# Testing for a wait once per run of V-product rounds, and no filler matmuls, in a one-core decode attention kernel

## The chip, the cores and the metric

The kernel runs on one core of a Trainium2 chip. The metric is device time in microseconds (us) for one execution. The profile's span, from the first to the last instruction, is some 1.4 to 2.8 us shorter than that. The core has a matrix engine (PE), a vector engine (DVE), a scalar engine (ACT), POOL, and SP, which here issues nearly all loads. The trace records the clock granted to PE, as 1 (full) or 0.5 (half); "mean clock" is its average over the span.

## The reference, cut to what matters

One token goes through layer norm, attention with grouped heads over a cache of 65,536 positions, a residual, a second layer norm and a gated feed-forward block. There are 32 query heads on 8 key and value heads of width 128.

```python
q = (layernorm(x) @ wq)                    # 32 heads of 128
scores = einsum("bhqd,bhkd->bhqk", q, k) * Dh ** -0.5
p = softmax(scores)                        # over 65536 positions
o = einsum("bhqk,bhkd->bhqd", p, v)        # the "V product"
h = x + o.reshape(...) @ wo
h2 = h + (sigmoid(g) * u) @ w_down         # g, u: layernorm(h) @ w_gate, w_up
```

K and V are 134 MB each in bf16, and each byte is used once.

## The kernel before

SP loads K and V in pieces of 8 or 12 chunks (4.19 or 6.29 MB) into one ring in SBUF, the on-chip memory. DVE transposes K, PE makes scores, ACT exponentiates, DVE transposes the probabilities, and PE makes the V product of head h-1 while the scores of head h are made. A load of a new piece is issued when the old contents of its place in the ring have been used, so a late PE or DVE makes a late issue.

PE's program is a loop over heads with four parts in each. Parts 0 and 3 hold rounds of the V product: ten and six rounds of eight matmuls. Three kinds of filler matmul, whose results nobody reads, keep PE occupied.

```python
def warm(e, n=1, load=True):               # n fillers of 128 x 504, into an unused bank of PSUM, where PE's results go
    ...
label("values", "part")
e.reg_mov(m, PARTS[0])                     # 10 rounds; part 3 sets 6
warm(e, 3)                                 # filler 1: ahead of each of the four parts
...
goto("sums", "values")
pv_regs(e)                                 # 14 address registers of this round
...
away("br_eq", p, c, "waits", waits, "products")   # in EVERY round: is a wait due?
goto("products", "sums")
section("B")                               # the 8 matmuls
mm_at(e, ps(5, 0, 504, 96, 128), ..., kept=True)  # filler 2: one in every round
e.reg_alu(p, p, s, ALU.add)
...
e.reg_alu(m, m, -1, ALU.add)
e.br_ne(m, 0, on_true="sums", on_false="sums_end")
label("sums_end")
def outs():
    warm(e, 2); section("O"); warm(e, 1, load=False)   # filler 3: around a head's output
```

The tests ask whether the next rounds need a V piece that may not have landed: after six rounds of part 0, and, for the last head only, after four of part 3.

## Time and profile before

| | kernel before |
|---|---|
| time, median of 6 runs | 657.7 us (657.62 to 659.03) |
| span of the profiled run | 656.2 us |
| bytes read, mean rate | 282.33 MB, 430 GB/s |
| PE busy, mean clock | 460.9 us, 0.872 |
| filler matmuls | 128 in the rounds, 121 elsewhere |

The times fall into two groups, near 657.6 and near 658.9 us.

This is the timeline of PE's weight loads in the last part of the last head. The columns are start in us, duration in us, engine, line, operation and operands, count, and in brackets the idle time before.

```profile
637.41 0.17 PEld L415 LDWEIGHTS PS<-ring,PT_sb 128*32 x8 [1.09 <-issue]
638.52 0.17 PEld L415 LDWEIGHTS PS<-ring,PT_sb 128*32 x8 [0.95 <-issue]
639.68 0.17 PEld L415 LDWEIGHTS PS<-ring,PT_sb 128*32 x8 [1.00 <-issue]
640.80 0.17 PEld L415 LDWEIGHTS PS<-ring,PT_sb 128*32 x8 [0.95 <-issue]
```

A round starts 1.11 to 1.16 us after the one before it. The eight weight loads take 0.17 us. "issue" means that the profile shows nothing that PE waited for: here its own sequencer works through registers and branches. In the round that starts at 469.29 us, for one, the trace records six register operations of 36 to 79 ns and two branches, of 226 and 75 ns.

### The profile page before, as it was taken

What the parts mean: (1) busy time and instruction counts of PE and PEld (TensorE: products, weight loads), DVE (VectorE), ACT (ScalarE), POOL (GpSimd) and SP (SyncE); (2) the same over time, 40 slices, a digit from 0 to 9 for tenths busy, and PEclk for the clock granted to TensorE, in tenths of its full rate; (3) what the DMA queues carried; (4) which work ended last, traced back from release to release, by engine and by line L of the source; (5) the groups of instructions that cost most, each with busy time, mean ns of one, the idle gap of its engine ahead of it and who ended that gap; (6) DMA issues with size and microseconds to landing.
All of it is one profiled execution on the core that took longest, in us unless ns stands there. A gap on an engine that the chain in (4) does not pass through costs nothing.

```text
span 656.2 us, 6578 instructions
## 1 busy us (share of the span) xinstructions
PE 460.9 (70%) x2564; PEld 73.8 (11%) x1587; DVE 350.2 (53%) x432; ACT 42.9 (7%) x114; POOL 3.6 (1%) x17
## 2 busy tenths in 40 slices
PE   0688587857669567786677676695767966777776
PEld 0200010011001010010100111010100101001122
DVE  1299846747266645647258380684536572573202
ACT  1100200020000200001000200002000020001001
POOL 1000000000000000000000000000000000000000
PEclk9989799788889697896887988787978978879798
DMA  9999999999999999999999999999999999999998
GB/s 400 431 447 431 425 421 431 431 437 433 455 431 431 431 415 434 440 443 433 421 447 431 431 423 447 446 434 437 399 447 431 431 431 431 460 434 411 425 429 348
DMA packets 8498, 282.33 MB, mean 430 GB/s; under 512 B 1073, under 2 KB 1074, under 8 KB 1586
## 3 DMA queue, kind: packets, MB, share of 16 engines
q1 hardware_dynamic: 8354, 282.33, 99.6%
q10 hardware_dynamic: 144, 0.00, 0.0%
HBM read 282.33 MB, written 0.00 MB: 430 GB/s over the span
## 4 chain that ended last, share of the span: by engine, by line
DMA 54%; PE 26%; DVE 12%; issue 6%; ACT 1%; PEldq 0%; PEld 0%; SPq 0%
DMA ring<-in_A_k_cache_dram 33%; PE PS L415 22%; DMA ring<-in_A_v_cache_dram 19%; DVE ktw L504 11%; DMA x_col<-in_A_x_dram 2%; PE PS L423 2%; ACT P_sb L550 1%; PE PS L817 0%; DVE PT_sb L560 0%; DVE M_sb L511 0%; PE PS L660 0%; PEldq L171 0%; PE PS L835 0%; PE PS L386 0%; PE PS L544 0%
## 5 line engine op out<-in xcount | busy, mean ns | idle before, releaser
L504 DVE STREAM_TRANSPOSE ktw<-ring 128x1024 f32<-128x1024 f32 x256 | 292.3, 1207 | 152.2 <-DMA ring<-in_A_k_cache_dram 152.2
L415 PE MATMUL PS<-ktw 128*128 128x512 bf16 x1024 | 287.1, 430 | 103.2 <-DVE ktw L504 86.0
L415 PE MATMUL PS<-ring,PT_sb 128*32 x1024 | 90.5, 423 | 52.6 <-PEq L171 26.8
L415 PEld LDWEIGHTS PS<-ktw 128*128 x256 | 26.7, 104 | 343.6 <-issue 246.4
L415 PE MATMUL PS<-qz,PT_sb 128*32 128x504 bf16 x128 | 53.1, 415 | 0.0
L415 PEld LDWEIGHTS PS<-ring,PT_sb 128*32 x1024 | 25.0, 115 | 134.7 <-issue 131.0
L593 ACT ACTIVATE po_sb<-PS,rl 128x512 bf16<-128x512 f32 x8 | 5.5, 687 | 524.1 <-PE PS L415 524.1
L423 PE MATMUL PS<-qz,ident 128*128 128x504 bf16 x121 | 33.7, 374 | 2.1 <-issue 2.1
L511 DVE TENSOR_REDUCE M_sb<-PS 128x1 f32<-128x512 f32 x32 | 19.9, 683 | 22.4 <-PE PS L415 22.4
L539 DVE TENSOR_REDUCE gmj<-PS 1x4 f32<-1x128 f32 x8 | 2.2, 279 | 46.0 <-PE PS L537 46.0
L550 ACT ACTIVATE P_sb<-PS,negmax 128x512 bf16<-128x512 f32 x32 | 21.6, 686 | 0.3
L560 DVE STREAM_TRANSPOSE PT_sb<-P_sb 128x512 bf16<-128x512 bf16 x32 | 20.1, 680 | 1.5 <-ACT P_sb L550 1.5
L386 PE MATMUL PS<-st,onesf 128*128 128x2 f32 x4 | 1.0, 312 | 17.1 <-DVE st L385 17.1
L415 PE MATMUL PS<-ring,xz 128*8 x32 | 9.6, 471 | 2.3 <-issue 2.3
L609 DVE TENSOR_TENSOR Lw<-O,blk_of 128x896 bf16<-128x896 bf16 (+1 forms) x2 | 1.4, 683 | 17.7 <-ACT O L599 17.7
L567 DVE TENSOR_REDUCE lsum<-PS 128x1 f32<-128x4 f32 x8 | 1.3, 162 | 17.6 <-PE PS L565 17.6
L415 PE MATMUL PS<-ktw,O 128*1 x26 | 7.5, 377 | 0.6
L423 PEld LDWEIGHTS PS<-qz,ident 128*128 128x128 bf16 x40 | 3.8, 96 | 35.3 <-issue 35.3
L544 PE MATMUL PS<-one_f,gmrep 1*128 1x1 f32 x16 | 3.2, 268 | 5.0 <-DVE gmrep L541 5.0
L468 DVE STREAM_TRANSPOSE qt<-qh 32x512 bf16<-32x512 bf16 x1 | 0.7, 700 | 11.0 <-ACT qh L465 11.0
L401 DVE CAST hT<-x_col 128x4 f32<-128x4 bf16 x1 | 0.2, 170 | 11.9 <-DMA x_col<-in_A_x_dram 11.9
L550 ACT ACTIVATION_READ_ACCUMULATOR P_sb<-PS,negmax 128x1 f32 x32 | 6.5, 203 | 0.0
(85 smaller groups left out, 73.9 us busy)
## 6 DMA issues: line engine op xcount, KB each, us to landing
ring<-in_A_k_cache_dram SPq DMA_DIRECT2D x16, 6144.0 KB, 24.4
ring<-in_A_v_cache_dram SPq DMA_DIRECT2D x15, 6144.0 KB, 24.9
ring<-in_A_v_cache_dram SPq DMA_DIRECT2D x9, 4096.0 KB, 29.6
ring<-in_A_k_cache_dram SPq DMA_DIRECT2D x8, 4096.0 KB, 24.7
ring<-in_A_wq_dram SPq DMA_DIRECT2D x1, 4096.0 KB, 12.3
ktw<-in_A_wo_dram SPq DMA_DIRECT2D x1, 3584.0 KB, 13.1
ring<-in_A_v_cache_dram SPq DMA_DIRECT2D x1, 2048.0 KB, 36.8
ring<-in_B_w_gate_dram SPq DMA_DIRECT2D x1, 1792.0 KB, 28.4
```

Source lines behind the costliest of these rows:

```text
L386: op("pe", lambda e: e.matmul(ps(bank, c0, c0 + 2), lhsT=onesf[:, :], rhs=st[i][:, :], start=True, stop=True), [f"st.{i}", f"sta.{i}", "on ...
L415: return e.add_instruction(mybir.InstMatmult(name=nc.get_next_instruction_name(), engine=mybir.EngineType.PE, ins=[rhs, lhsT], outs=[e.low ...
L423: e.add_instruction(mybir.InstMatmult(name=nc.get_next_instruction_name(), engine=mybir.EngineType.PE, ins=[e.lower_ap(qz[:, 0:504]), e.lo ...
L504: op("dve", lambda e, d=dst, sr=src: e.transpose(d, sr), deps, f"T{b}.{c}", to="T")
L511: op("dve", lambda e, u=u: e.tensor_reduce(M_sb[:, u % 4:u % 4 + 1], ps(u % NS, 0, 512), AX.X, ALU.max), [f"S{b}.{NC - NR + k}"], f"mx{u}" ...
L539: op("dve", lambda e: e.tensor_reduce(gmj[:, :], ps(MISC, 0, 128, 0, 1).rearrange("p (i a c) -> p a i c", a=4, c=NC), AX.XY, ALU.max), [f" ...
L544: op("pe", lambda e: e.matmul(ps(MISC, 128, 129), lhsT=gmrep[0:1, :], rhs=one_f[0:1, 0:1], start=True, stop=True), [f"gmrep{h}"], f"neg{h}")
L550: op("act", lambda e, b=b: e.activation(P_sb[:, (b % 4) * 512:(b % 4 + 1) * 512], ps(b % NS, 0, 512), AF.Exp, bias=negmax[:, k:k + 1], sca ...
L560: op("dve", lambda e, b=b: e.transpose(PT_sb[:, (b % 4) * 512:(b % 4 + 1) * 512], P_sb[:, (b % 4) * 512:(b % 4 + 1) * 512]), [f"E{b}"], f" ...
L567: op("dve", lambda e: e.tensor_reduce(lsum[:, :], ps(MISC, 132, 136), AX.X, ALU.add), [f"l{h}"], f"ls{h}", to="D")
L593: op("act", lambda e: e.activation(po_sb[:, :], ps(PO, 0, 512), AF.Copy, scale=rl[:, :]), [f"PV{h}.{NR - 1}", f"rl{h}"], f"po{h}", to="po")
L609: op("dve", lambda e: e.tensor_tensor(Lw[i][:, :].rearrange("p (j c) -> p j c", j=n), bass.AP(tensor=O2, offset=j0, ap=[[NQ, 128], [1, n], ...
```

## The change

The intent is to give PE less to do. The rounds go in runs: six then four, or four then two. The register `m` counts the rounds of the run and `k` holds the length of the next run. The test for a wait stands at the end of a run and no longer in the round, and all 249 fillers go. The core of the diff (removed definitions and renamed targets are cut):

```diff
-            e.reg_mov(m, PARTS[0])
-            warm(e, 3)
+            e.reg_mov(m, 6)
+            e.reg_mov(k, 4)
...
-            e.reg_mov(m, PARTS[3])
+            e.reg_mov(m, 4)
+            e.reg_mov(k, 2)
...
             def waits():
-                e.reg_alu(c, c, 8, ALU.add)
+                e.reg_alu(m, k, 0, ALU.add)
+                e.reg_mov(k, 0)
...
-            away("br_eq", p, c, "waits", waits, "products")
-            goto("products", "sums")
             section("B")
-            mm_at(e, ps(5, 0, 504, 96, 128), ..., True, 32, 96, kept=True)
...
             e.br_ne(m, 0, on_true="sums", on_false="sums_end")
             label("sums_end")
-            def outs():
-                warm(e, 2)
-                section("O")
-                warm(e, 1, load=False)
-            away("br_eq", w, w0 - 12, "outs", outs)
+            away("br_ne", k, 0, "waits", waits, "sums")
+            away("br_eq", w, w0 - 12, "outs", lambda: section("O"))
...
-        op("pe", lambda e: warm(e, 1, load=False))
```

More of the change, by code (lines that the diff above doesn't have):

```diff
@@ L418, in mm_at @@
                 bass_skip_group_check=True, **more))
-        def warm(e, n=1, load=True):
-            for i in range(n):
-                more = dict(ldweights=False) if i or not load else {}
-                e.add_instruction(mybir.InstMatmult(
-                    name=nc.get_next_instruction_name(), engine=mybir.EngineType.PE, ins=[e.lower_ap(qz[:, 0:504]), e.lower_ap(ident[:, :])],
-                    outs=[e.lower_ap(ps(5, 0, 504))], start_tensor_calc=True, stop_tensor_calc=True, tile_size=(128, 128),
-                    tile_position=(0, 0), bass_skip_group_check=True, **more))
         regs, R, here = [], {}, OrderedEngineSet([mybir.EngineType.PE])
@@ L668, in away @@
                 label(f"{name}_not")
-            i, w, p, v, m, c, s = (R.setdefault(n, e.alloc_register(f"r_{n}")) for n in "iwpvmcs")
+            i, w, p, v, m, k, s = (R.setdefault(n, e.alloc_register(f"r_{n}")) for n in "iwpvmks")
             w0, p0 = addr_of(ktw, W0 + NC - 1 + 127), addr_of(PT_sb, 31 * 4)
@@ L681, in pe_flow @@
             e.reg_mov(p, p0)
-            e.reg_mov(c, p0 + 6)
             e.reg_alu(v, i, v_at[0], ALU.min)
@@ L711, in waits @@
             def waits():
-                e.reg_alu(c, c, 8, ALU.add)
+                e.reg_alu(m, k, 0, ALU.add)
+                e.reg_mov(k, 0)
                 e.br_eq(w, w0, on_true="second", on_false="fourth")
                 label("second", "waits")
-                away("br_eq", i, i_last, "rows_of_o", last_second, "products")
+                away("br_eq", i, i_last, "rows_of_o", last_second, "sums")
                 section("V2")
-                nc.br("products", engines=here)
+                nc.br("sums", engines=here)
                 label("fourth", "waits")
-                e.br_ne(i, i_last, on_true="products", on_false="last_rounds")
+                e.br_ne(i, i_last, on_true="sums", on_false="last_rounds")
                 label("last_rounds", "fourth")
                 section("VL")
-            away("br_eq", p, c, "waits", waits, "products")
-            goto("products", "sums")
             section("B")
-            mm_at(e, ps(5, 0, 504, 96, 128), at_reg(PT_sb, reg(e, 11), [[PT_ROW, 128], [4, 32]]), e.lower_ap(qz[:, 0:504]), True, 32, 96, kept=True)
             e.reg_alu(p, p, s, ALU.add)
```

## The prediction

> **What bounds the kernel now.** I read the page's slices and queues first, then the groups, the DMA issues, the windows by head, and last the timeline of the tail. The slices and queues settle most of it:
>
> ```profile
> PEclk9989799788889697896887988787978978879798
> DMA  9999999999999999999999999999999999999998
> ...
> q1 hardware_dynamic: 8354, 282.33, 99.6%
> ...
> HBM read 282.33 MB, written 0.00 MB: 430 GB/s over the span
> ```
>
> The DMA engines are busy from the first slice to the last, so the span of 656.2 us is 282.33 MB over 430 GB/s. The question for any change on PE is only whether it lets this queue run dry, or whether it ends work that comes after the last byte.
>
> The landing records of the trace give the queue's pace: one 6.29 MB piece lands 14.49 us after the one before it, in every head (529.73, then 544.22 us), which is 434 GB/s. They also give the slack. At each issue I subtract the issue time from the landing of everything issued earlier. The smallest backlog in heads 1 to 7 after the start-up is 9.4 us (the V piece issued at 365.61 us after the second late round of the V product; the data before it lands at 375.0). Issues that wait for the score matmuls by way of DVE have 9.8 us, the others 10 to 20. The start-up has 6.8 us, the first load of the output weight at 602.5 us has 4.6. The DMA issues say the same in another way:
>
> ```profile
> ring<-in_A_k_cache_dram SPq DMA_DIRECT2D x16, 6144.0 KB, 24.4
> ring<-in_A_v_cache_dram SPq DMA_DIRECT2D x15, 6144.0 KB, 24.9
> ```
>
> Last column: us from issue to landing. A piece needs 14.5 us for itself, so it typically waits some 10 us behind others.
>
> The windows, one for each head from one K issue to the next, show an engine with room:
>
> ```profile
> core 0: us, PE busy (x) PEld busy (x) DVE busy (x) ACT busy (x) POOL busy (x), PEclk, DMA share, GB/s
> 350.75:428.07 77.32, 55.51 (x297) 7.89 (x175) 42.42 (x50) 4.68 (x13) 0.00 (x0) 0.85 1.00 433
> 428.07:505.48 77.41, 55.47 (x297) 7.75 (x175) 42.34 (x50) 4.68 (x13) 0.00 (x0) 0.85 1.00 435
> ```
>
> PE is busy 55 of 77 us, fillers included, at a mean clock of 0.85.
>
> **The tail** is the one place where PE might count. The chain of waits gives almost all of 578 to 656 us to PE and this tempts one to think every filler there is time. The timeline shows what the end waits for:
>
> ```profile
> 641.28 0.38 PE L415 MATMUL PS<-qz,PT_sb 128*32 128x504 bf16 x1
> 642.84 0.15 PEld L415 LDWEIGHTS PS<-ring,PT_sb 128*32 x8 [1.88 <-issue]
> 642.85 0.63 PE L415 MATMUL PS<-ring,PT_sb 128*32 x8 [1.19 <-issue]
> ...
> 648.82 2.74 PE L817 MATMUL PS<-ring,hc 128*1 128x448 bf16 x32 [0.25 <-DVE hc L804]
> ...
> 653.25 1.01 PE L835 MATMUL PS<-ring,hhT 128*1 128x128 bf16 x56 [0.97 <-DVE hhT L830]
> ```
>
> Of the 56 last matmuls, the single records show 48 started by 653.87 us and the last eight at 653.98, just after the last piece of the down weight landed (653.93). What follows (copies, output DMA) is fixed: 656.2. So the end is set by the last landing, with the compute chain arriving only some 0.06 us before it. Compute that gets faster gains nothing; compute that gets slower in the tail is seen at once.
>
> [...] The clock records here are 1 or 0.5 only, in multiples of 3.41 us[...]. [...] here four of a round start within 10 ns, the next four 0.23 us later. [...] here the one that closes a round takes 226 ns, the one that asks for the wait and falls through 75 ns, some 115 ns with the gap to the next matmul.
>
> **The change part by part.** The groups of filler matmuls (after the bar, busy us and mean ns of one, then idle time before):
>
> ```profile
> L415 PE MATMUL PS<-qz,PT_sb 128*32 128x504 bf16 x128 | 53.1, 415 | 0.0
> L423 PE MATMUL PS<-qz,ident 128*128 128x504 bf16 x121 | 33.7, 374 | 2.1 <-issue 2.1
> ```
>
> (1) Filler in each round of the V product, 128 of them. A round is 1.14 us from start to start (469.29, 470.46, 471.57, 472.73, 473.85 us). At full clock the array needs 3 x 0.215 us of it, while the sequencer needs all of it: from the first weight load, 0.37 us to the closing branch, 0.28 us to the first register operation, 0.37 us of these, 0.12 us for the branch to the next load. The filler ends before the next round's matmuls, so at full clock taking it out saves nothing. At half clock three passes need 3 x 0.43 = 1.29 us, more than the sequencer, and two need 0.86; there a round falls from about 1.25 to about 1.05 us.
>
> (2) The test for a wait goes from every round to the end of a run: one branch of 0.115 us fewer, so a round of about 1.03 us. 16 rounds give 16 x 0.115 = 1.8 us for a head. The branches that lead to a wait (0.22 us each, three of them, the 1.19 us of idleness at 642.85) are still paid once a run, but now before the data have landed where they are late.
>
> (3) Three fillers ahead of each of a head's four parts: 4 x 0.64 = 2.6 us. The fillers around the head's output lie beside the 0.69 us of ACT that PE waits for; I count 0.
>
> Sum: 1.8 + 2.6 = 4.4 us of PE time for a head, 35 us over 8 heads. All of heads 1 to 7 is off the path: what they issue earlier only waits longer in a full queue. Worth for the time: 0.
>
> (4) In the tail the V piece lands at 636.22 and PE is at that moment in three fillers; rounds start at 637.42. Without fillers and with the register work done, they start at about 636.8. Four rounds of 1.03 end before the last V piece lands (641.08); the last two start after the landing, a branch of 0.2 and 0.4 us of registers, at about 641.8 where they now start at 642.85. Everything up to the gate matmuls moves ahead by about 1.1 us. The last up weight lands at 649.66 and the last down weight at 653.93 as before, so the gain turns into waiting. Worth: 0 to 0.1 us.
>
> (5) What it costs: activity for the clock. A round keeps the array streaming 0.43 of 1.03 us, not 0.65 of 1.14, and waits for data are no longer padded. I expect a mean clock of 0.7 to 0.85 instead of 0.87 (a guess: the profile shows no threshold). A score matmul costs 0.215 us more at half clock. To make the queue dry, PE must be late by 9.4 us, which is 44 cold score matmuls between a K piece's landing and the issue; a whole K piece of 12 chunks has 48, and PE streams them without pause when behind, which brings the clock back, as in the 32 that take 6.94 us (0.217 each) after the cold start at 582.79. [...] In the tail, cold rounds, cold small matmuls and twelve cold groups of four in the down product (0.62 us warm, 1.3 cold) could add 0.4 + 0.3 + 0.6 us against the 1.1 gained: -0.1 to +0.5 us at the end.
>
> Sum: 658.9 (median before) + 0 (heads) - 0.1 to +0.5 (tail); I choose 658.8, because the tail has its 1.1 us to spend first.
>
> **The rivals.** (a) The clock falls for long stretches, PE becomes the bound: at half clock a head needs 128 x 0.43 = 55 us of scores, 16 x 1.05 = 17 of rounds, some 5 for the softmax: 77 us, as long as the stream's 77.4. Even then it hardly loses; a few us a head would be 670 to 680. For it: fillers were put there by someone. Against it: 9.4 us of backlog that is renewed in every head. 2%. (b) The chain of waits is right and the PE tail is the path: 4 parts x 0.64 and 16 rounds x 0.115 come off, 4 us, 655. Against it: the eight matmuls at 653.98, and the landings after 606, which run without a gap. Even so, under 1%, still within 2%. (c) The tail alone is cold: 659.5. About 15%.
>
> **Range and chances.** The three runs before spread from 657.6 to 659.0, wider than any effect that I expect; with (c) upward the range is 657.4 to 660.2. 2% is 13 us; the stream of bytes forbids it downward, only (a) gives it upward: 0.01, 0.97, 0.02.
>
> **What would show it.** Right: DMA share still 99%, 6.29 MB each 14.5 us, no gap between landings, last landing within 0.3 us of 653.9; rounds of about 1.03 us; PE busy down by some 40 to 60 us, less if cold; clock below 0.87; idle time ahead of the last eight matmuls grown to near 1 us. Wrong: backlog at some issue falling to zero with a gap between landings (rival a), a last landing well before 653 (b), or last matmuls starting well after the last landing (c).

In the printed text, comparisons with rules and figures that no trace of this case shows are cut; the measurements beside them are left. ("The one that closes a round" there is a compare-and-branch.)

The trace of the kernel before: by the median, score matmuls start 0.217 us apart at full clock and 0.427 at half. In each half-clock stretch before the last, PE had streamed for 2.2 to 5.6 us when the clock came back (at 582.79 us, the case in part (5), it starts to stream in a half-clock stretch that ends at 587.85). By these figures I estimate that a cold start costs up to 13 x 0.21 = 2.7 us, within the 9.4 us of backlog. The half-clock rounds of part (1) can be read too: 1.27 us in before, and 0.97 to 1.03 in nearly all rounds of the changed kernel.

## The result, and the profile after

The changed kernel takes 657.59 us (median of 6 runs, 657.56 to 658.86) against 657.7 us. The ratio is 0.9996 with a 95% interval of 0.9983 to 1.0009: the same. Ratios are the mean time of one kernel's runs over that of the other's of the same rounds, so not quite the ratio of the medians quoted. Executions over 1.5% slower than the fastest of the same kernel are left out of the means.

The slices of the page for the changed kernel, with the granted clock in tenths of full speed and the busy share of the DMA engines:

```profile
PEclk9989789877779587786787777785868967878757
DMA  9999999999999999999999999999999999999998
```

The stream is as full as before, and the clock is lower in most slices from the sixth on. The windows of two heads say it in numbers:

```profile
core 0: us, PE busy (x) PEld busy (x) DVE busy (x) ACT busy (x) POOL busy (x), PEclk, DMA share, GB/s
350.60:428.00 77.40, 50.94 (x267) 7.11 (x171) 42.43 (x50) 4.68 (x13) 0.00 (x0) 0.76 1.00 434
428.00:505.40 77.40, 51.69 (x267) 7.18 (x171) 42.33 (x50) 4.68 (x13) 0.00 (x0) 0.76 1.00 434
```

PE is busy some 4 us less in a head, at a clock of 0.76 instead of 0.85, and the head takes the same 77.4 us. The rounds in the same place as those shown of before:

```profile
636.71 0.16 PEld L415 LDWEIGHTS PS<-ring,PT_sb 128*32 x8 [6.57 <-issue]
637.68 0.16 PEld L415 LDWEIGHTS PS<-ring,PT_sb 128*32 x8 [0.81 <-issue]
638.70 0.16 PEld L415 LDWEIGHTS PS<-ring,PT_sb 128*32 x8 [0.86 <-issue]
639.67 0.16 PEld L415 LDWEIGHTS PS<-ring,PT_sb 128*32 x8 [0.81 <-issue]
```

They start 0.97 to 1.02 us apart. The 6.57 us ahead of the first are not a loss: PE waits there for a V piece that landed at 636.11 us. The rest of the tail, to be held against the tail lines in the prediction:

```profile
641.64 0.63 PE L415 MATMUL PS<-ring,PT_sb 128*32 x8 [1.32 <-DMA ring<-in_A_v_cache_dram]
...
647.55 3.15 PE L803 MATMUL PS<-ring,hc 128*1 128x448 bf16 x32 [0.25 <-DVE hc L790]
...
652.41 1.86 PE L821 MATMUL PS<-ring,hhT 128*1 128x128 bf16 x56 [0.98 <-DVE hhT L816]
653.88 0.10 PEld L821 LDWEIGHTS PS<-ring,hhT 128*1 128x1 bf16 x8 [0.31 <-DMA ring<-in_B_w_down_dram]
```

The last two rounds start 1.21 us earlier than before (641.64 against 642.85), the gate product 1.27 us earlier, the down product 0.84 us earlier. Then the last eight matmuls wait for the last piece of the down weight, which landed at 653.84 us (before: 653.93). Of the 1.27 us gained at the gate product, 0.43 go on the way to the down product and 0.51 in its first 48 matmuls, both with the array at half clock (its last stretch, from 646.6 us on); the 0.33 that are left go in that wait. The span is 656.2 us as before.

### The profile page after: what moved, and what is told of

It reads as the page before. It is cut to its first block, busy times and chain, and to the rows that moved or that the text cites. A ratio compares the mean times of both kernels' runs of the same rounds, so it can differ in the third digit from the quotient of the medians.

```text
span 656.2 us, 6240 instructions
## 1 busy us (share of the span) xinstructions
PE 428.9 (65%) x2315; PEld 69.3 (11%) x1547; DVE 350.2 (53%) x432; ACT 42.9 (7%) x114; POOL 3.6 (1%) x17
## 4 chain that ended last, share of the span: by engine, by line
DMA 61%; DVE 18%; PE 16%; issue 4%; ACT 1%; SPq 0%; PEldq 0%
DMA ring<-in_A_k_cache_dram 30%; DMA ring<-in_A_v_cache_dram 29%; DVE ktw L496 17%; PE PS L415 14%; DMA x_col<-in_A_x_dram 2%; PE PS L803 0%; ACT P_sb L542 0%; DVE M_sb L503 0%; PE PS L821 0%; PE PS L386 0%; PEldq L171 0%; DVE hh L813 0%; SPq L324 0%; SPq L342 0%; PE PS L617 0%
## 5 line engine op out<-in xcount | busy, mean ns | idle before, releaser
L415 PE MATMUL PS<-ring,PT_sb 128*32 x1024 | 100.2, 494 | 64.6 <-PEq L171 42.7
L415 PEld LDWEIGHTS PS<-ring,PT_sb 128*32 x1024 | 20.7, 116 | 142.5 <-issue 140.9
L386 PE MATMUL PS<-st,onesf 128*128 128x2 f32 x4 | 1.2, 364 | 17.2 <-DVE st L385 17.2
L536 PE MATMUL PS<-one_f,gmrep 1*128 1x1 f32 x16 | 4.7, 357 | 5.0 <-DVE gmrep L533 5.0
L529 PE MATMUL PS<-identf,gm 128*1 128x128 f32 x16 | 3.9, 333 | 5.6 <-issue 3.4
L588 PE MATMUL PS<-sel_bf,po_sb 128*128 128x4 bf16 x32 | 2.1, 169 | 6.3 <-ACT po_sb L585 6.3
```

Of the source, the lines that this page charges most:

```text
L415: return e.add_instruction(mybir.InstMatmult(name=nc.get_next_instruction_name(), engine=mybir.EngineType.PE, ins=[rhs, lhsT], outs=[e.low ...
L529: op("pe", lambda e: e.matmul(ps(MISC, 0, 128, 0, 1), lhsT=gm[:, :], rhs=identf[:, :], start=True, stop=True), [f"gm{h}"], f"gmT{h}", to="Q")
L536: op("pe", lambda e: e.matmul(ps(MISC, 128, 129), lhsT=gmrep[0:1, :], rhs=one_f[0:1, 0:1], start=True, stop=True), [f"gmrep{h}"], f"neg{h}")
L588: op("pe", lambda e, t=t: e.matmul(ps(OX, 0, 4), lhsT=po_sb[:, t * 128:(t + 1) * 128], rhs=sel_bf[:, 8 * t:8 * t + 8:2], start=(t == 0), s ...
```

## The experiments

Twelve kernels ran. "Backlog" is, as in the prediction, the time from the issue of a load to the landing of everything issued before it. The landing of a load is the last of the sixteen completions that the trace records for it.

### 1 and 2: each half of the change alone

The first is the kernel before with its fillers taken out:

```diff
-            warm(e, 3)
...
-            mm_at(e, ps(5, 0, 504, 96, 128), ..., kept=True)
...
-                warm(e, 2)
                 section("O")
-                warm(e, 1, load=False)
...
-        op("pe", lambda e: warm(e, 1, load=False))
```

> The kernel before without its 249 filler matmuls, the test for a wait still in every round. Theory (queue bound, both parts hidden): within 0.2% of before, span 656.1 to 656.3 us, last landing 653.8 to 654.0. Rounds stay near 1.10 us, because at full clock the sequencer and not the array sets them; mean clock as low as in the changed kernel, 0.77 to 0.81, because the fillers alone held it up. Smallest backlog in the heads between 9.4 us (before) and 11.0 (changed). Rival (the branch did nothing, the filler was the length of a round): rounds fall to 1.0 us here already.

Measured: 657.81 us against 657.86 for before, ratio 1.0001 (0.9985 to 1.0018). The median time between the last matmuls of two neighbouring rounds is 1.117 us (1.132 in before, 0.973 in the changed kernel), so the filler was not the length of a round. The mean clock is 0.775. The V loads after part 3 have backlogs of 10.7 to 11.2 us. One figure was missed: the span of the profiled run is 656.8 us, and that of the other three 656.4, not 656.1 to 656.3. The timeline of this run's tail shows where the 0.6 us are, at the gate product and the down product:

```profile
648.38 3.16 PE L812 MATMUL PS<-ring,hc 128*1 128x448 bf16 x32 [0.25 <-DVE hc L799]
...
653.23 1.66 PE L830 MATMUL PS<-ring,hhT 128*1 128x128 bf16 x56 [0.97 <-DVE hhT L825]
```

The last landing is at 653.89 us, as ever. But the down product begins at 653.23 us, as in before, and at half clock takes 1.66 us, against 1.01 in before. Here the end is set by PE: without fillers the tail is cold, that is, largely at half clock (mean 0.60 from 640 us on, against 0.89 in before), and the longer rounds leave nothing to pay for that.

The second is the changed kernel with all fillers put back in their places:

```diff
+            warm(e, 3)
...
             section("B")
+            mm_at(e, ps(5, 0, 504, 96, 128), ..., kept=True)
...
+                warm(e, 2)
                 section("O")
+                warm(e, 1, load=False)
...
+        op("pe", lambda e: warm(e, 1, load=False))
```

> The changed kernel with all 249 fillers put back: the written-out runs alone. Theory: within 0.2% of before, span 656.1 to 656.3 us; mean clock back at 0.86 to 0.89; rounds 1.00 to 1.05 us (one branch of about 0.115 us fewer). Rival (filler was the length of a round): rounds stay at 1.12 us.

Measured: 657.9 us, ratio 1.0002 (0.9986 to 1.0019), span 656.2 us, mean clock 0.866, rounds 1.00 us apart by the median. So taking the branch out shortens a round by 0.13 us, and the fillers hold the clock (0.866, against 0.79 in the changed kernel). Neither moves the time. The smallest backlog at the V loads is 8.9 us. The down product of this run shows best what the end waits for, as the chain comes early here and the down product is at full clock:

```profile
652.28 0.62 PE L837 MATMUL PS<-ring,hhT 128*1 128x128 bf16 x32 [1.10 <-DMA ring<-in_B_w_down_dram]
653.39 0.40 PE L837 MATMUL PS<-ring,hhT 128*1 128x128 bf16 x16 [0.49 <-DMA ring<-in_B_w_down_dram]
654.02 0.28 PE L837 MATMUL PS<-ring,hhT 128*1 128x128 bf16 x8 [0.24 <-DMA ring<-in_B_w_down_dram]
```

PE waits in turn for the three pieces of the down weight (landed at 652.15, 653.35 and 653.98 us).

### 3 and 4: half of V, to take the stream off the end

If the queue hides what PE gains, the gain must appear when there is less to load. Both kernels load only half the columns of each V piece and use stale data for the rest:

```diff
             a, z = cols or (j0, j1)
+            if k == "V":
+                z = (a + z) // 2
```

Their outputs are wrong, which doesn't matter for the times. The comparison with the reference does not notice attention's share of the output, so "correct" says little about V in this problem.

> The kernel before with half the columns of every V piece loaded, so wrong results on purpose: 67.1 MB fewer of 282.3, which at 434 GB/s is 154 us, so a queue bound of about 502 us. With 58 us of stream for a head, PE (55 us busy with its fillers, plus its waits) becomes the bound. Theory: 510 to 545 us, DMA share clearly under 99%. Rival (queue still the only bound): 500 to 505 us.

> The changed kernel with the same halved V loads, wrong results on purpose. Theory (the change frees about 4.4 us of PE a head, and the full queue hides it): 5 to 35 us faster than the kernel before with halved loads. Rival (the lower clock eats what the missing fillers give): within 3 us of it, or slower.

Measured: 571.28 us for before, 554.07 us for the changed kernel, 17.2 us less. That lies in the range expected of the theory and rules out its rival. The level was missed: 571, not 510 to 545. The stream was not off the path: the view of waits has DVE waiting 48.7 us for K pieces in the first run and 47.0 in the second, and the DMA share was still 90% and 92%. So it may have covered part of the difference. Hence the next three.

### 5, 6 and 7: half of K and V

```diff
             a, z = cols or (j0, j1)
+            if (k, h) != ("K", 0):
+                z = (a + z) // 2
```

(A first build that halved head 0's K too was refused before it ran: it read memory that nothing had written.) The same edit was made in the kernel before, in the one without fillers, and in the changed one.

> The kernel before with half the columns of every V piece and of every K piece but head 0's unloaded, so wrong results on purpose: some 156 MB, 360 us of stream at 434 GB/s. With half the V loads alone the queue was still busy 90%, so it may still have covered some of the difference; here it should not. Theory: compute alone sets the time, 535 to 570 us.

> The same halved loads, the kernel before without its fillers (tests in every round). By the working of the prediction, 2.6 us a head: about 21 us faster than the kernel before with these loads. If the clock eats part of it, 5 to 15 us.

> The same halved loads, the changed kernel. By the working of the prediction, 4.4 us a head: 35 us faster than the kernel before with these loads, 14 us faster than the one without fillers. From the halved V loads alone, where the change gave 17.2 us: about 17 to 25 us if part of the PE time stays hidden beside DVE or is given back by the lower clock.

Measured, four runs each: 541.12, 548.12 and 526.65 us. Their ratios to the same runs of the full kernel before are 0.8217, 0.8328 and 0.8002, each with an interval of about 0.002 either way (1.3 us), so the differences are clear of noise. In all three, every K and V piece landed at least 0.7 us before DVE or PE first used it, and the view of waits has none for K or V any more, so compute alone sets the time here, at 541 us for the kernel before, as expected. From the three pages (span, PE's busy time, granted clock by slice), the kernel before:

```profile
span 539.9 us, 6578 instructions
...
PE 415.7 (77%) x2564; PEld 71.3 (13%) x1587; DVE 349.5 (65%) x432; ACT 42.9 (8%) x114; POOL 3.6 (1%) x17
...
PEclk9989979999899979998999989997999989997988
```

The kernel without fillers:

```profile
span 545.9 us, 6289 instructions
...
PE 392.3 (72%) x2315; PEld 68.7 (13%) x1547; DVE 349.5 (64%) x432; ACT 42.9 (8%) x114; POOL 3.6 (1%) x17
...
PEclk9979968898889968995989887995989687995766
```

The changed kernel:

```profile
span 525.0 us, 6240 instructions
...
PE 380.9 (73%) x2315; PEld 67.4 (13%) x1547; DVE 349.5 (67%) x432; ACT 42.9 (8%) x114; POOL 3.6 (1%) x17
```

This overturns a term of the sum. Taking out the fillers takes 23.4 us of busy time from PE (415.7 to 392.3) and makes the kernel 7.0 us slower. The mean clock falls from 0.942 to 0.845, and the matmuls that remain last longer: those of the V product 457 ns on average instead of 400, the score matmuls 405 instead of 396. (That the clock is the reason is read from these durations; no run changed the clock alone.) Putting the rounds in runs gives 21.5 us (548.12 to 526.65), which is 0.17 us for each of the 128 rounds, with all that follows from it. The change as a whole gives 14.5 us when compute is the bound, all of it from the runs, where 17 to 25 or 35 were expected.

### 8 and 9: how late PE may be

Here the changed kernel gets 20 or 70 more matmuls ahead of the late rounds of every head but the last. In the iteration where `i` equals `i_last`, the V product is that of the last head, so it is left out:

```diff
             label("values3")
+            away("br_ne", i, i_last, "late", lambda: warm(e, 20))   # or 70
```

> The changed kernel with 20 more matmuls (4.3 us at full clock, up to 8.6 at half) ahead of the late rounds of heads 0 to 6, so that PE is late in each. Smallest backlog of the changed kernel in the heads is 9.8 us, and 11.0 to 11.3 us at the V load that waits for these rounds. Theory: the stream has no gap, the backlog at that V load falls to 4 to 7 us, and the time stays within 0.2% of before. Rival (PE is on the path): 7 x 4.3 = 30 us longer.

> The same with 70 more matmuls, 15.1 us at full clock. Theory: 15.1 is 3.8 to 4.1 us more than the backlog of 11.0 to 11.3 us, so the queue runs dry once a head, with a gap of 3.8 to 6 us each time (the start of a transfer included): over six or seven heads 25 to 42 us longer, 683 to 700 us. Rival (some other slack, or none): no change, or the whole 7 x 15 = 106 us.

With 20 the V loads of the heads kept backlogs of 6.4 to 7.0 us, and no landing in heads 0 to 6 was late, as the theory has it. But the span was 659.0 us, 2.8 more (657.9 in the second run), and the time 659.93 us, a ratio of 1.0027 (0.9986 to 1.0068), where within 0.2% was expected. The landings fell behind only after the issue of the output weight at 604.6 us. Experiment 10 takes this up.

With 70 the time was 712.54 us, 55 us more, above the 683 to 700 expected. At the V load of each head the queue had been empty for 3.7 to 4.2 us when the issue came, as expected from 15 us against 11. But the landing then came 6.7 to 7.7 us late and not 4 to 6, six times, and 11.3 us late at the output weight, where the queue had been empty for 8.7. (The start of a transfer, which the expectation counts in, shows as some 0.7 to 1.0 us: in the kernel before, the first load is issued at 0.00 us and its packets start at 1.02, the output at 654.95 and 655.69. The rest of the width up to 6 was an estimate.) Those seven make 54 us; experiment 10 comes to the rest. So a queue that ran dry here cost about 3 us (2.6 to 3.6) on top of the time it was empty. The windows of this run at the first of these places:

```profile
core 0: us, PE busy (x) PEld busy (x) DVE busy (x) ACT busy (x) POOL busy (x), PEclk, DMA share, GB/s
144.00:150.00 6.00, 5.01 (x46) 0.72 (x32) 0.00 (x0) 0.00 (x0) 0.00 (x0) 1.00 0.44 131
150.00:165.00 15.00, 8.65 (x40) 1.64 (x29) 10.11 (x12) 4.68 (x13) 0.00 (x0) 0.66 0.93 402
```

In the 6 us after the queue ran dry (last landing 144.12 us) the stream moves 131 GB/s, and over the next 15 us 402, not 434. Of the runs with all bytes loaded, only this one has the time that PE lost in the heads on the path: the slack that the prediction read from the landings is real.

### 10: the same lateness, but not at the output weight

```diff
-            away("br_ne", i, i_last, "late", lambda: warm(e, 20))
+            away("br_ne", i, i_last, "late",
+                 lambda: away("br_ne", i, i_last + lag, "late2", lambda: warm(e, 20)))
```

> The changed kernel with 20 more matmuls ahead of the late rounds of heads 0 to 5, but not of head 6, whose late rounds release the load of the output weight. The run with them in heads 0 to 6 lost 2.8 us, and its landings fell behind only after the output weight's issue at 604.6 us, with 2.6 us of backlog left there; the V loads of the heads kept 6.4 us or more and lost nothing. Theory: all of the 2.8 us came from that one issue, so span 656.1 to 656.4 us here and V-load backlogs of 6.3 to 7.1 us. Rival (lateness in the heads costs time by some other way): 658 to 659 us.

Measured: span 657.5 us (657.4 in the second run), in neither range. The V loads of the heads had 6.6 to 7.0 us of backlog and no landing of heads 0 to 6 was late, so lateness in the heads does cost nothing. The 1.3 us are in one place: the load after the two of the output weight, a V piece with 15.5 us of backlog at its issue, landed at 627.85 us where the changed kernel has 626.39. Of its sixteen completions, the first came at 626.03 us (626.07 in the changed kernel) and only the last was late, by about 1.4 us. Part 3 of this run's page has a row, the last, that the changed kernel has not (its own row of instructions is one packet of 80 bytes, at the start):

```profile
q1 hardware_dynamic: 8354, 282.33, 99.4%
q10 hardware_dynamic: 144, 0.00, 0.0%
q8 instruction: 1, 0.02, 0.0%
```

It is a single packet of 16,384 bytes of instructions, recorded at 619.94 us for 0.92 us, while that V piece was streaming. It goes with a delay of the stream, which has no room (99.4% of the engines' span): one completion is late, and the stream is still behind at the end. The last eight matmuls, which wait for the last piece of the down weight, start at 655.21 us here and at 653.88 in the changed kernel.

The run with 20 matmuls in all heads before it had the same packet, at 625.18 us, and the same V piece 1.57 us late. Its other 1.30 us were at the output weight, issued with 2.62 us of backlog left: of the sixteen completions twelve were on time, four 0.3 to 1.4 us behind them. Together 2.9 us, which is its 2.8. So, as far as one run shows, the output weight's load needs more than 2.6 us of backlog. With 4.64 us in the kernel before it lost nothing.

The run with 70 matmuls is a third case, and one in which lateness plays no part. It has such a packet at 95.19 us, before the first of the 70 matmuls (131.75 us). The K piece that streamed then landed 1.29 us late, again by one completion of the sixteen (100.69 us, the others by 99.43). In the run with 20 the same K piece met no packet and was on time (99.41 us). With these 1.29 us the 54 of that run become the 55 measured. That the packet delays the stream remains a coincidence, in three runs of three in which one fell in the full stream; no run took it away on purpose.

### 11 and 12: an earlier last landing

Six of the 14 rows of the down weight are not loaded (wrong results), in both kernels:

```diff
         for i, (r0, r1) in enumerate(WD_SPLIT):
             at = AT["wd"] * CH
+            r1 = 2 if i == 0 else r1
```

> The kernel before with 6 of the 14 rows of the down weight left unloaded, wrong results on purpose: 0.79 MB fewer, so the last landing comes 1.8 us earlier, near 652.1 us. Theory: the compute chain of before had only some 0.06 us to spare, so it now sets the end and the span falls by 0.05 to 0.2 us to 656.0 to 656.15. Rival (end follows the stream): 1.8 us less, 654.4.

> The changed kernel with the same rows left out, wrong results on purpose. Its chain reaches the down product 0.84 us earlier, but the array is at half clock there, so 56 matmuls take about 1.5 us instead of 0.8. Theory: the span falls by 0.15 to 0.35 us, to 655.85 to 656.05, little more than in the kernel before. Rival (clock of no matter there): falls by 0.8 us or more.

The last landing came at 652.07 us and 652.32 us, the first figure 1.86 us earlier than before. The spans of the profiled runs were 655.5 us in the kernel before and 656.0 us in the changed one (656.5 and 656.6 in the second runs). Neither follows the landing by 1.8 us, so the compute chain is close behind it in both. The sizes did not come as expected. In the kernel before, the gate product and the down product:

```profile
648.25 1.74 PE L818 MATMUL PS<-ring,hc 128*1 128x448 bf16 x32 [0.25 <-DVE hc L805]
...
652.65 0.95 PE L836 MATMUL PS<-ring,hhT 128*1 128x128 bf16 x56 [2.24 <-DVE hhT L831]
```

In the changed kernel:

```profile
648.28 3.16 PE L804 MATMUL PS<-ring,hc 128*1 128x448 bf16 x32 [0.25 <-DVE hc L791]
...
653.14 0.95 PE L822 MATMUL PS<-ring,hhT 128*1 128x128 bf16 x56 [0.97 <-DVE hhT L817]
```

In the kernel before, the gate product starts 0.57 us earlier than in its first profile (648.82), as the last two rounds do (642.28 against 642.85): PE was through its fillers when the V piece landed at 636.17 us, where in the first profile it went into three of them after the landing. That the gate product took 1.74 us instead of 2.74 gained next to nothing, as from its start to the down product are 4.40 us here and 4.43 there. In the changed kernel the gate product starts 0.73 us later than in its first profile (647.55): 0.30 is a later landing of the last V piece (641.27 us against 640.97), the rest a stretch of half clock that falls on the last rounds here (from the start of the last round to the first ACT instruction after it are 1.11 us, against 0.68 there). Its down product, slow in its first profile, was fast here. So the chain's arrival moves by 0.6 to 0.7 us from run to run. What the changed kernel can spare in the tail is known no closer than that. These two runs support the claim that landing and chain arrive together; they do not give its 0.06 us.

## Why the prediction was right or wrong

**The bound (right).** The stream of bytes sets the time. Every landing kept its pace in both kernels. Lateness of PE changed it in two cases only: 15 us of it in a head, and the 20 matmuls ahead of the output weight's load, which left a backlog of 2.6 us.

**The number (right within the range, and off by the base).** The prediction added at most half a microsecond to 658.9 us. That base was the median of three runs, two of which were in the upper of the two groups. Six runs give 657.7. The change itself was put at -0.1 us and came out at -0.1; that is far below what the runs can tell apart (0.9983 to 1.0009 is -1.1 to +0.6 us), so this agreement is luck.

**Parts (1) and (2): the fillers in the rounds and the branch (right in kind; the branch was mis-sized).** Experiments 1 and 2 separate them: fillers out, 1.132 to 1.117 us; branch out, 1.132 to 1.00; both, 0.973. The prediction had 0.115 us for the branch and rounds of about 1.03. (Of its parts of a round, the first, from weight load to closing branch, is 0.34 us by the records and not 0.37, the register work some 0.40; the sum is right.) The branch and its gaps are worth 0.13 to 0.14 us by the median, and 0.17 us a round in time where compute is the bound.

**Part (3): three fillers ahead of each part, 4 x 0.64 = 2.6 us of a head (wrong).** This term took busy time for length. With the stream out of the way, removing all fillers costs 7.0 us over the whole kernel instead of saving some 21. (No run took out these fillers and left those in the rounds.) The prediction had put the clock under costs in part (5), but never subtracted it from the sum of 4.4 us for a head. That sum, 35 us in all, measured 14.5 where compute is the bound, 1.8 for a head. It did no harm to the number, because all of it was multiplied by zero: hidden under the queue.

**Part (4): the tail (right in its end; the gain went elsewhere).** Rounds at 636.7 (636.8 predicted), the last two at 641.64 (641.8), the gate product 1.27 us earlier (1.1), nothing gained at the end. The prediction had the gain turn into waiting; 0.3 us of it did, and 0.9 us went to the half clock, which part (5) had as a risk. That the chain must hurry and the last landing decides was the right reading; the chain of waits, which laid nearly the whole tail on PE, was misleading.

**Part (5): the clock (right in its direction, with two sizes off).** The mean fell to 0.79, within 0.7 to 0.85. The backlog of the heads grew: the smallest after the start-up is 9.8 us, where before has 9.4. But "idle time ahead of the last eight matmuls grown to near 1 us" failed: it is 0.31 us by the weight-load line. The array spent the rest at half clock. PE's busy time fell by 32 us (460.9 to 428.9), less than the 40 to 60 named, as the prediction had said for a colder array. How busy PE must be to hold the clock is not shown: the mean clock of the profiled runs under a full stream is 0.866 to 0.872 with all fillers and 0.775 to 0.79 without. The 4.6 us at the output weight were also worth less than they look, as a backlog of 2.6 us already lost 1.3 us. The changed kernel issues that load with 6.9 us.

**Rival (a), the queue runs dry,** was rightly set aside: this took 70 extra matmuls a head. **Rival (b), PE's tail is the path,** is refuted by the wait for the last landing, clearest in experiment 2. **Rival (c), a cold tail,** did not befall the change, but it is what the profiled run of experiment 1 shows, 0.6 us. In the change, the runs brought the chain forward by enough to pay for the cold.

No experiment points to a version that beats both kernels by an amount that the times could show: the end follows the last landing, and what PE gains is hidden by the stream.

## What to carry to other kernels

Where a stream of loads never pauses, first write down the backlog at each issue, from the landing records, and treat compute that leaves a margin of it as free, in both directions (here 4.6 us left was enough, 2.6 was not). Do not count a filler matmul as its busy time: here 23.4 us of fillers fell partly into waits and went with a higher clock for their neighbours (0.942 against 0.845, with half of K and V), and the kernel without them was 7.0 us slower, so try it with the stream made smaller on purpose. And look at what arrives last, not at which engine the chain of waits names.
